# Float16 attention scores from tile 18 on, and five moves of DVE and ACT work, in a windowed attention with a SiLU MLP

## The chip, the cores and the metric

One core of a Trainium2 chip runs the kernel. The metric is the device time of one execution in microseconds, the median over several runs. The engines are TensorE (PE, its weight loads PEld), VectorE (DVE), ScalarE (ACT), GpSimd (POOL) and SyncE (SP), which issues the transfers here.

## The reference

Attention over 8 batches, 8 heads, 576 tokens, 64 numbers a head, with a causal window of 128 tokens and a bias that falls linearly with the distance; then a two-layer MLP with SiLU, from 512 to 2048 and back, over the 8 × 576 = 4608 tokens. Inputs and output are float32.

```python
scores = scale * np.matmul(q, k.transpose(0, 1, 3, 2))        # scale = 1/8
bias = slopes[:, None, None] * (-np.abs(rel))[None, :, :]
mask = (rel >= 0) & (rel < window)                            # window = 128
scores = np.where(mask, scores + bias[None], -1000000000.0)
scores = scores - np.max(scores, axis=-1, keepdims=True)
attn = np.exp(scores)
attn = attn / (np.sum(attn, axis=-1, keepdims=True) + 1e-09)
x = np.matmul(attn, v)           # (B, H, S, D), then to (4608, 512)
h = x @ w_in
g = h * (1.0 / (1.0 + np.exp(-h)))
out = g @ w_out
```

## The kernel before

**Tiles.** The tokens make 36 tiles of 128. Two batches (1152 tokens) are nine tiles, so four "two-batches" b = 0 to 3 follow each other; the first tile of each has no tile before it and only half of the score blocks (`blocks`), and the fifth is cut between two batches (`other_batch`, L301 to 308). A pair p is half of a tile's heads: i, q = divmod(p, 2), 72 pairs in all. A pair has two halves u of two heads h each.

**A pair's steps.** `scores` (L286 to 299): float32 matmuls of 64 rows, the two heads of a half on the two halves of the rows, 8 a full pair and 4 in a first tile; a float32 matmul leaves two records in the trace, so the profile counts x16 and x8. `row_max` (L310 to 319, one half u a call): a custom DVE instruction scales the scores by −0.125, subtracts the bias table `tab` and keeps the minimum of the negated scores. `exps` (L321, ACT). `p_hi` (L334, ACT) and `p_lo` (L339, DVE) split the probabilities into two float16 parts, `p_transpose` (L347) turns them by a DMA. `attend` (L372 to 387): 24 float16 matmuls of 65 columns, products of two-part values. `normalize` (L398 to 412, DVE), `x_hi` (L422, ACT) and `x_lo` (L124, DVE) give the MLP's input in two float16 parts, which another DMA transposes; for the first four tiles PE transposes it (`x_transpose`, L434 to 439), and their probabilities too (L357 to 368).

**The MLP.** Nine groups g of 512 tokens (4 tiles, 8 pairs), 16 slices f of 128 hidden columns each, n = 16 g + f. `gemm1` (two halves, L489 in float16 from g = 2, L494 before) gives h; SiLU is `act1` (tanh, ACT L502), `act2` (DVE L507), `act3` (ACT L515 or, in float16, L517: gh), `act4` (DVE L523 or POOL L122: the low part gl); `gemm2` (two halves, L555, gl last of each three) sums over the slices into four output banks, and `store` (L560 to 568) empties these at a group's end, each through a buffer, "io" for the first two, and to memory. "io" has two buffers.

**Weights.** They come as 64-bit numbers. `w_next` starts one slice of one weight: `w_split1`, `w_low3` (ACT L585, L592), and at the next three positions `w_join` (DVE L597), `w_hi` (ACT L607), `w_lo` (POOL). 32 such pieces are taken one after another, three ahead of the main loop, the others at half 0 of each step of g = 0. Later `w_stat` finds each weight's largest number, and `conv1`, `conv2`, `conv3` (ACT L635, DVE L641 and L647) turn each of 32 slices to two-part float16, a slice each four positions; `conv2`'s result takes an "io" buffer, too.

**Scales.** Each two-batches' values are scaled by a power of two: `vscale_load` and `vscale_reduce` (L156, L168, L171) take the largest of nine chunks, and `vscale_finish` (L184 to 213) combines them in three stages (a reduction over a row; a PE transpose L193 and small DVE steps L195 to 206; a PE broadcast L209 and a copy). The values then go to two float16 parts by `v_hi` (POOL L266) and `v_lo` (DVE L277), which `attend` reads.

**The order.** Every engine works in the order in which the program issues. A group has 64 positions: two halves of `gemm1` and `gemm2` of each slice; a negative position lies ahead of the main loop. `put(position, step)` and `later` fill a plan (L657 to 733), and `begin` issues what is due ahead of each position's matmuls. A pair's `scores` stand at n = `at(p)`, 8 p − 78 for p ≥ 16, so a pair each eight positions; the others are offsets from it: row maxima at n + 1 and n + 2, `attend` at n + 13 in the steady part.

Of the kernel before, what the change touches and what calls it, by code (L numbers as in the profile page):

```python
# [78 lines left out]
def tile_window_attention_then_silu_mlp(ctx, tc, qk, v, w_in, w_out, base8, out):  # L79
# [79 lines left out]
    def vscale_reduce(b, i):  # L159
        t = vred[b][i]  # L160
        if i == 0:
            vred[b]["m"] = pool.tile([P, VCH], F32, tag="vm", name=f"vmx{b}")
# [21 lines left out]
    def vscale_finish(b, stage):  # L184

        r, name = vred[b], "".join(str(c) for c in b) if isinstance(b, tuple) else b
# [3 lines left out]
        elif stage == 1:  # L190
# [16 lines left out]
        else:  # L207
            ps = ps_of(next_tag("misc"), f"vs{name}")
            nc.tensor.matmul(ps[:, 0:2], ones[:1, :], r["col"][:1, 1:3], start=True, stop=True)  # L209
# [36 lines left out]
    ks, qs, rvs, st = {}, {}, {}, {}  # L246

# [44 lines left out]

# [17 lines left out]
    def row_max(p, u):  # L310
        q, o = p % 2, blocks(p)
        n = (o.stop - o.start) * P
        st[p]["t"][u] = t = pool.tile([P, 2, 2 * P], F32, tag="t", bufs=3, name=f"t{p}_{u}")
        for h in range(2):
            nc.vector.tensor_tensor_reduce(  # L315
                out=t[:, h, 2 * P - n :], in0=st[p]["sp"][h][:, u, o].rearrange("p o c -> p (o c)"),
                in1=tab[:, 4 * q + 2 * u + h, 2 * P - n :], scale=-0.125, scalar=3.0e38,
# [344 lines left out]
    for p in range(NPAIR):  # L662
# [8 lines left out]
        else:  # L671
            a = n + (2 * STEP + 2 if p < 2 * GT else 15 if p < 4 * GT else 13)
# [4 lines left out]
        put(n + 2, row_max, p, 1)  # L677
# [27 lines left out]
        if q == 0:  # L705
            if i > 1:
# [8 lines left out]
    for x in range(3):  # L715
        for which in range(2):
# [153 lines left out]
```

## Time and profile before

| | |
|---|---|
| median of 3 runs | 969.84 us (969.56 to 971.48) |
| the profiled execution | 973.28 us |
| its span, first to last instruction | 971.5 us |
| mean granted PE clock | 0.988 of full speed |
| PE busy | 938.7 us |
| DVE, ACT, POOL busy | 597.0, 497.3, 141.6 us |

The page and the views give one profiled execution. In the timeline each row is a start, a busy time, an engine, a line, an operation, out<-in by the program's names, partitions × elements and a count; in brackets stands how long the engine was idle just before and what ended that. A row of matmuls merges neighbours, and its busy time includes the fill at the end, so that spacing is read from start to start. In a view of windows "PEclk" is the share of full clock that was granted. In a view of waits a row has the waiting engine and line, what it waited for, the total, how often, and the longest.

### The profile page before, as it was taken

How to read it: one execution, taken by the hardware profiler on the slowest of the kernel's cores; microseconds unless marked ns; L12 is line 12 of the kernel's file. 1: busy time of each engine (PE TensorE's matmuls, PEld its weight loads, DVE VectorE, ACT ScalarE, POOL GpSimd, SP SyncE). 2: the span in 40 equal slices, each digit the busy share in tenths (PEclk: the TensorE clock that was granted, in tenths of full speed). 3: DMA queues.
4: the chain of work that ended last, by engine and by line, in shares of the span. 5: the costliest groups of instructions: out<-in, count | busy, mean ns of one | idle time of the engine just before them, and what ended most of it. 6: DMA issues, size and time to landing. Idle time of an engine off the chain costs nothing.

```text
span 971.5 us, 17272 instructions
## 1 busy us (share of the span) xinstructions
PE 938.7 (97%) x6572; PEld 578.0 (59%) x6572; DVE 597.0 (61%) x1535; ACT 497.3 (51%) x1016; POOL 141.6 (15%) x129
## 2 busy tenths in 40 slices
PE   7989899999989999999999999999999999999998
PEld 5866677777768887544545554554555555544443
DVE  4867886656768877877566656555555565543222
ACT  4688877775544544555454445444544454433222
POOL 3146655122112222000000000000000000000000
PEclk8999999999998999999999999999999999999999
DMA  7949982333353542433364535333434343231001
GB/s 233 305 143 220 252 233 58 88 77 77 76 137 102 111 109 66 120 80 78 93 157 117 118 87 125 87 83 77 129 83 85 86 126 84 63 55 54 1 1 44
DMA packets 201075, 104.95 MB, mean 108 GB/s; under 512 B 168224, under 2 KB 176416, under 8 KB 200992
## 3 DMA queue, kind: packets, MB, share of 16 engines
q1 hardware_dynamic: 200992, 103.84, 42.1%
q8 instruction: 52, 0.85, 0.4%
q14 instruction: 31, 0.25, 0.1%
HBM read 54.00 MB, written 9.44 MB: 65 GB/s over the span
## 4 chain that ended last, share of the span: by engine, by line
PE 84%; DVE 5%; DMA 4%; ACT 4%; issue 2%; SPq 1%; POOL 0%; ACTq 0%; DVEq 0%; POOLq 0%
PE o L555 33%; PE h L489 30%; PE sp L295 7%; PE h L494 7%; PE av L385 5%; DMA vm<-v 1%; DMA early<-v 1%; DVE v L277 1%; DVE t L315 1%; DMA hl<-hr 1%; DVE gt L507 1%; DVE wm L597 1%; DMA wr<-w_out 1%; ACT gt L502 1%; PE pt L357 1%
## 5 line engine op out<-in xcount | busy, mean ns | idle before, releaser
L555 PE MATMUL o<-w,gh 128*128 128x512 f16 (+1 forms) x1152 | 351.7, 387 | 0.3 <-ACT gh L515 0.3
L489 PE MATMUL h<-xt,w 128*128 128x512 f16 (+1 forms) x1536 | 318.0, 355 | 0.0
L502 ACT ACTIVATE gt<-h,gsc 128x512 f32<-128x512 f32 x112 | 77.0, 687 | 319.6 <-PE h L489 317.6
L555 PE MATMUL o<-w,gl 128*128 128x512 f16 (+1 forms) x576 | 221.7, 385 | 1.5 <-POOL gl L122 1.5
L489 PEld LDWEIGHTS <-w 128*128 128x128 f16 x1536 | 143.8, 98 | 130.9 <-issue 2.4
L507 DVE SCALAR_TENSOR_TENSOR gt<-gt,h 128x512 f32<-128x512 f32 x144 | 98.6, 685 | 179.3 <-ACT gt L502 179.0
L555 PEld LDWEIGHTS <-gh 128*128 128x128 f16 x768 | 74.8, 98 | 88.6
L325 ACT ACTIVATE t<-t,mx 128x256 f32<-128x256 f32 (+1 forms) x288 | 121.4, 485 | 7.6 <-DVE mx L315 7.6
L315 DVE CUSTOM_DVE_ANT_0 t<-sp,tab 128x256 f32<-128x256 f32 (+1 forms) x288 | 102.2, 402 | 18.4 <-PE sp L295 18.0
L523 DVE SCALAR_TENSOR_TENSOR gl<-gt,gh 128x512 f16<-128x512 f32 x96 | 66.4, 691 | 75.0 <-ACT gh L517 74.9
L339 DVE SCALAR_TENSOR_TENSOR hr<-t,hr 128x512 f16<-128x512 f32 (+1 forms) x128 | 93.4, 747 | 24.4 <-ACT hr L334 24.4
L494 PE MATMUL h<-xh,w 128*128 128x512 f32 x256 | 91.6, 412 | 4.1 <-ACT xh L438 3.2
L266 POOL TENSOR_SCALAR v<-rv,vsc 128x512 f16<-128x512 f32 x32 | 26.7, 834 | 443.0 <-DMA rv<-v 311.7
L295 PEld LDWEIGHTS sp<-k,q 64*128 64x128 f32 x1088 | 69.4, 192 | 30.8 <-issue 30.1
L295 PE MATMUL sp<-k,q 64*128 64x128 f32 x1088 | 83.8, 291 | 3.6 <-DVE xs L412 3.5
L122 POOL TENSOR_TENSOR gl<-gt,gh 128x512 fp32r<-128x512 f32 x45 | 60.1, 1336 | 185.2 <-ACT gh L515 142.8
L517 ACT ACTIVATE gh<-gt 128x512 f16<-128x512 f32 x96 | 60.0, 625 | 47.5 <-DVE gt L507 47.2
L555 PEld LDWEIGHTS o<-w,gh 128*128 128x128 f32 x384 | 69.9, 188 | 16.5 <-ACT gh L515 1.2
L334 ACT ACTIVATE hr<-t 128x512 f16<-128x512 f32 (+1 forms) x128 | 75.9, 598 | 3.2 <-DMA hl<-hr 3.2
L385 PEld LDWEIGHTS <-hl 128*128 128x128 f16 x1632 | 58.7, 98 | 26.2 <-issue 15.4
L385 PE MATMUL av<-v,hl 128*128 128x65 f16 (+1 forms) x1632 | 63.3, 194 | 9.9 <-DVE mx L315 5.5
L555 PEld LDWEIGHTS <-gl 128*128 128x128 f16 x384 | 37.5, 98 | 47.8 <-DVE gl L523 3.5
(99 smaller groups left out, 786.6 us busy)
## 6 DMA issues: line engine op xcount, KB each, us to landing
q<-qk SPq DMA_DIRECT2D x36, 256.0 KB, 3.0
k<-qk SPq DMA_DIRECT2D x36, 256.0 KB, 3.1
out<-ot SPq DMA_DIRECT2D x36, 256.0 KB, 2.4
wr<-w_in SPq DMA_DIRECT2D x16, 512.0 KB, 6.6
wr<-w_out SPq DMA_DIRECT2D x16, 512.0 KB, 6.2
rv<-v SPq DMA_DIRECT2D x32, 256.0 KB, 2.9
vm<-v SPq DMA_DIRECT2D x27, 256.0 KB, 3.2
early<-v SPq DMA_DIRECT2D x9, 256.0 KB, 6.1
```

What stands on the lines that cost most here:

```text
L295: nc.tensor.matmul(sp[h][:, u, o], qs[i][rows, 2 * q + u], ks[i - 1 + o][rows, 2 * q + u], start=True, stop=True, skip_group_check=True,)
L315: nc.vector.tensor_tensor_reduce(out=t[:, h, 2 * P - n :], in0=st[p]["sp"][h][:, u, o].rearrange("p o c -> p (o c)"), in1=tab[:, 4 * q + 2 ...
L325: nc.scalar.activation(x, x, AF.Exp, bias=st[p]["mx"][:, 2 * u + h : 2 * u + h + 1], scale=-1.0)
L334: nc.scalar.activation(split_of(p, u, hr)[:, 0], t[:, :, 2 * P - n :], AF.Copy, scale=PSCALE)
L339: nc.vector.scalar_tensor_tensor(out=hr[:, 1], in0=t[:, :, 2 * P - n :], scalar=PSCALE, in1=hr[:, 0], op0=ALU.mult, op1=ALU.subtract)
L385: nc.tensor.matmul(av[:, 2 * u + h, : rhs.shape[-1]], lhs, rhs, start=(n == 0), stop=(n == len(seq) - 1), skip_group_check=True,)
L489: nc.tensor.matmul(o, w[:, wp, cc], x, start=start and k == 0, stop=stop, skip_group_check=True)
L494: nc.tensor.matmul(hps[n], w[:, cc], x, start=(half == 0 and i == 0), stop=(half == 1 and i == len(seq) - 1), skip_group_check=True,)
L502: nc.scalar.activation(gt, hps[n], AF.Tanh, scale=scale)
L507: nc.vector.scalar_tensor_tensor(out=gt, in0=gt, scalar=1.0, in1=hps[n], op0=ALU.add, op1=ALU.mult)
L523: nc.vector.scalar_tensor_tensor(out=gl, in0=gt, scalar=CUT, in1=gh, op0=ALU.mult, op1=ALU.subtract)
L555: nc.tensor.matmul(ops[ti], a[:, t], w, start=(f == 0 and i == 0), stop=(f == NF - 1 and i == len(seq) - 1), skip_group_check=True,)
```

## The change

1. From tile 18 on (p ≥ 36, b = 2 and 3) the scores are float16 products. A second input `qk16` holds q and k with each head's 64 rows on both halves of the partitions. `load_qk16` brings both for a pair (512 KB) at n − 18. `hi16` (ACT, n − 10 for q, n − 8 for k) scales them into float16, `lo16` (DVE, n − 6 and n − 5) takes the rest: for q into the upper 64 rows of the same tile, for k into a second one. A score block is then two matmuls of 128 rows, q's hi and lo against k's hi, and against k's lo: 16 matmuls of 128 columns for a full pair instead of 8 float32 ones. The scale of q and k goes into the bias table, which is multiplied once for each of the two two-batches (`rescale_bias`), and into the row maximum's scale, now a column.
2. For these scales `qk_load` and `qk_sum` (ACT, two sums of absolute values each) read the q and k of b = 2 and 3 ahead of time, and `scales16` combines them with the values' scale. The old loads of q and k from tile 18 on are gone.
3. `row_max` of the second half stands at n + 1, right behind the first's, for p ≥ 8.
4. The first three `w_next` stand at −25, −17 and −10 instead of −19, −7 and −2, and the fourth one position later.
5. The conversions of slices above 4 come three positions later (`CLEAR`).
6. The stages of the scales stand at 0, +2 and +5 instead of 0, +1 and +2; the two weights' scales share their instructions (`wscale_finish`).
7. `attend` stands at n + 12 instead of n + 13 for p ≥ 36.

The core of the diff:

```diff
+QK16 = 2
+CLEAR = 3
...
+    def qk_sum(b, i):
+        t = vred.pop((b, "qk", i))
+        for k in range(2):
+            m = vred[b]["m"][:, (1 + k) * VCH + i : (1 + k) * VCH + i + 1]
+            nc.scalar.activation(t[:, k], t[:, k], AF.Abs, accum_out=m)
...
+    def rescale_bias(b):
+        ratio = vsc[b][:, 8:9] if b > QK16 else vsc[b][:, 7:8]
+        flat = tab.rearrange("p h c -> p (h c)")
+        nc.vector.tensor_scalar_mul(flat, flat, ratio)
...
+    def load_qk16(p):
+        i, q = divmod(p, 2)
+        raw16[p] = t = pool.tile([P, 2, 4, P], F32, tag=RAW16[p % 2], bufs=1, name=f"r16_{p}")
+        nc.sync.dma_start(t, qk16[i - QK16 * NBLK, q])
...
+        nc.scalar.activation(out16, raw16[p][:, k], AF.Copy, scale=scale)
...
+        rows = slice(D, P) if k == 0 else slice(0, P)
+        hi, lo = (q16[p], q16[p]) if k == 0 else (k16[i][:, q, 0], k16[i][:, q, 1])
+        nc.vector.scalar_tensor_tensor(
+            out=lo[rows], in0=raw16[p][rows, k], scalar=vsc[i // NBLK][rows, 2 + 2 * k : 3 + 2 * k], in1=hi[rows],
+            op0=ALU.mult, op1=ALU.subtract,
+        )
...
+                if i >= QK16 * NBLK:
+                    for h in range(2):
+                        for part in range(2):
+                            nc.tensor.matmul(
+                                sp[h][:, u, o], q16[p][:, 2 * u + h], k16[i - 1 + o][:, q, part, 2 * u + h],
+                                start=part == 0, stop=part == 1, skip_group_check=True,
+                            )
+                    continue
...
+        scale = vsc[b][:, 6:7] if b >= QK16 else -0.125
...
-            a = n + (2 * STEP + 2 if p < 2 * GT else 15 if p < 4 * GT else 13)
+            a = n + (2 * STEP + 2 if p < 2 * GT else 15 if p < 4 * GT else 13 if i < QK16 * NBLK else 12)
+        if i >= QK16 * NBLK:
+            put(n - 18, load_qk16, p)
+            put(n - 10, hi16, p, 0)
+            put(n - 8, hi16, p, 1)
+            put(n - 6, lo16, p, 0)
+            put(n - 5, lo16, p, 1)
+            if block_of(i) == 0 and q == 0:
+                put(n, rescale_bias, i // NBLK)
...
-        put(n + 2, row_max, p, 1)
+        put(n + (2 if p < 2 * GT else 1), row_max, p, 1)
...
+    for x, wait in enumerate((0, 2, 5)):
+        put(STATS + 2 * NF + 2 + wait, wscale_finish, x)
...
-                put(n + SLICE * f + (k if which or f else 0), fn, which, f)
+                put(n + SLICE * f + (CLEAR if f > 4 else 0) + (k if which or f else 0), fn, which, f)
...
+            if b >= QK16:
+                put(n - 52 + 5 * i, qk_load, b, i)
+                put(n - 46 + 5 * i, qk_sum, b, i)
...
-        for n in (-19, -7, -2):
+        for n in (-25, -17, -10):
...
-                if g == 0 and half == 0:
+                if g == 0 and half == (n == 0):
```

On PE before, the scores of pair 40 (tile 20), between a `gemm2` and a `gemm1`; sp40_0 and sp40_1 are the banks of the two heads, k19 and k20 the tiles of k:

```order
L555 MATMUL o3_3_4974<-w16_1_5_5232,gl59_5641 128x512
L295 MATMUL sp40_0_5725<-k19_5080,q20_5352 128x128
L295 MATMUL sp40_1_5726<-k19_5080,q20_5352 128x128
L295 MATMUL sp40_0_5725<-k20_5354,q20_5352 128x128
L295 MATMUL sp40_1_5726<-k20_5354,q20_5352 128x128
L295 MATMUL sp40_0_5725<-k19_5080,q20_5352 128x128
```

The same place on PE after:

```order
L682 MATMUL o3_3_4991<-w16_1_5_5330,gl59_5713 128x512
L413 LDWEIGHTS q16_40_5622
L413 MATMUL sp40_0_5801<-k16_19_5382,q16_40_5622 128x128
L413 LDWEIGHTS q16_40_5622
L413 MATMUL sp40_0_5801<-k16_19_5382,q16_40_5622 128x128
L413 LDWEIGHTS q16_40_5622
L413 MATMUL sp40_1_5802<-k16_19_5382,q16_40_5622 128x128
L413 LDWEIGHTS q16_40_5622
L413 MATMUL sp40_1_5802<-k16_19_5382,q16_40_5622 128x128
```

Each float32 matmul has become two float16 ones into the same bank, each with its own weight load; the place in the order is the same.

On DVE before, at the row maxima of pair 15 (g = 0); wm10_1 is the weight piece being joined, gt10 the SiLU of slice 10:

```order
L315 ISA t15_0_1790,mx15_1775<-sp15_0_1765,tab_65 128x256
L315 ISA mx15_1775 128x1
L315 ISA t15_0_1790,mx15_1775<-sp15_1_1766,tab_65 128x256
L315 ISA mx15_1775 128x1
L597 SCALAR_TENSOR_TENSOR wm10_1_1787<-wm10_1_1787,wr10_1_1361 128x512
L315 ISA t15_1_1809,mx15_1775<-sp15_0_1765,tab_65 128x256
L315 ISA mx15_1775 128x1
L315 ISA t15_1_1809,mx15_1775<-sp15_1_1766,tab_65 128x256
L315 ISA mx15_1775 128x1
L507 SCALAR_TENSOR_TENSOR gt10_1807<-gt10_1807,h10_1780 128x512
```

The same on DVE after:

```order
L442 ISA t15_0_1790,mx15_1775<-sp15_0_1765,tab_65 128x256
L442 ISA mx15_1775 128x1
L442 ISA t15_0_1790,mx15_1775<-sp15_1_1766,tab_65 128x256
L442 ISA mx15_1775 128x1
L442 ISA t15_1_1793,mx15_1775<-sp15_0_1765,tab_65 128x256
L442 ISA mx15_1775 128x1
L442 ISA t15_1_1793,mx15_1775<-sp15_1_1766,tab_65 128x256
L442 ISA mx15_1775 128x1
L724 SCALAR_TENSOR_TENSOR wm10_1_1787<-wm10_1_1787,wr10_1_1364 128x512
L634 SCALAR_TENSOR_TENSOR gt10_1810<-gt10_1810,h10_1780 128x512
```

The join has moved from between the two halves of the maxima to behind them.

On DVE before, at the end of g = 1; ot1_1 and ot1_3 are output tiles, wr16_0_5 and w16_0_2 belong to the conversion of slice 5 of the first weight, xs24 and x12 to the attention of tile 12:

```order
L565 TENSOR_SCALAR ot1_1_3446<-o1_1_2391 128x512
L339 SCALAR_TENSOR_TENSOR hr25_1_3427<-t25_1_3403,hr25_1_3427 128x512
L641 SCALAR_TENSOR_TENSOR wr16_0_5_3477<-w0_5_1188,vscw0_2999,w16_0_2_3370 128x512
L565 TENSOR_SCALAR ot1_3_3488<-o1_3_2409 128x512
L403 TENSOR_SCALAR r24_3491<-av24_3449 128x4
L404 RECIPROCAL r24_3491<-r24_3491 128x4
L647 SCALAR_TENSOR_TENSOR w16_0_2_3370<-w0_5_1188,vscw0_2999,wr16_0_5_3477 128x512
L412 TENSOR_TENSOR xs24_3510<-av24_3449,r24_3491 128x256
```

The same on DVE after:

```order
L692 TENSOR_SCALAR ot1_1_3433<-o1_1_2391 128x512
L466 SCALAR_TENSOR_TENSOR hr25_1_3415<-t25_1_3371,hr25_1_3415 128x512
L692 TENSOR_SCALAR ot1_3_3473<-o1_3_2409 128x512
L530 TENSOR_SCALAR r24_3476<-av24_3436 128x4
L531 RECIPROCAL r24_3476<-r24_3476 128x4
L539 TENSOR_TENSOR xs24_3496<-av24_3436,r24_3476 128x256
L130 SCALAR_TENSOR_TENSOR x12_3513<-xs24_3496,x12_3513 128x256
L768 SCALAR_TENSOR_TENSOR wr16_0_5_3527<-w0_5_1188,vscw_3046,w16_0_2_3358 128x512
```

The conversion's second step has moved from ahead of the normalizing of pair 24 to behind it.

More of the change, by code (lines that the diff above doesn't have):

```diff
@@ L184, in vscale_finish @@
     def vscale_finish(b, stage):
[L186 removed]
+        if b >= QK16:
+            scales16(b, stage)
+            return
+        r, name = vred[b], b
         if stage == 0:
@@ new lines, in rescale_bias, with wscale_finish @@
+    def rescale_bias(b):
+        ratio = vsc[b][:, 8:9] if b > QK16 else vsc[b][:, 7:8]
+        flat = tab.rearrange("p h c -> p (h c)")
+        nc.vector.tensor_scalar_mul(flat, flat, ratio)
+    def wscale_finish(stage):
+        if stage == 0:
+            vred["w", "col"] = col = pool.tile([P, 3], F32, tag="vcol", name="vcolw")
+            for k in range(2):
+                nc.vector.tensor_reduce(col[:, k : k + 1], vred["w", k]["m"], axis=AX.X, op=ALU.max)
+        elif stage == 1:
+            ps = ps_of(next_tag("misc"), "vtw")
+            for k in range(2):
+                nc.tensor.transpose(ps[:1, k * P : (k + 1) * P], vred["w", "col"][:, k : k + 1], ident)
+            vred["w", "row"] = row = pool.tile([P, 9], F32, tag="row", bufs=1, name="roww")
+            c, inv = row[:1, 0:2], row[:1, 2:4]
+            ci = c.bitcast(I32)
+            nc.vector.tensor_reduce(c, ps[:1, : 2 * P].rearrange("p (k i) -> p k i", k=2), axis=AX.X, op=ALU.max)
+            nc.vector.tensor_single_scalar(ci, ci, 0x7F800000, op=ALU.bitwise_and)
+            nc.vector.tensor_single_scalar(ci, ci, 1, op=ALU.logical_shift_right)
+            nc.vector.tensor_single_scalar(ci, ci, 0x1FC00000, op=ALU.add)
+            nc.vector.tensor_single_scalar(ci, ci, 0x7F800000, op=ALU.bitwise_and)
+            nc.vector.tensor_single_scalar(inv.bitcast(I32), ci, -(14 << 23), op=ALU.add)
+            nc.vector.tensor_scalar(ci, ci, -1, 268 << 23, op0=ALU.mult, op1=ALU.add)
+        else:
+            ps = ps_of(next_tag("misc"), "vsw")
+            nc.tensor.matmul(ps[:, 0:4], ones[:1, :], vred["w", "row"][:1, 0:4], start=True, stop=True)
+            t = pool.tile([P, 4], F32, tag="wsc", bufs=1, name="vscw")
+            nc.vector.tensor_copy(t, ps[:, 0:4])
+            for k in range(2):
+                wsc["w", k] = t.rearrange("p (s k) -> p k s", k=2)[:, k]
```

94 lines of the change are left out of this document (75 added, 19 removed).

## The prediction

> **What bounds the kernel now.** I read the page first: the busy shares, the granted clock and the chain that ended last.
>
> ```profile
> span 971.5 us, 17272 instructions
> PE 938.7 (97%) x6572; PEld 578.0 (59%) x6572; DVE 597.0 (61%) x1535; ACT 497.3 (51%) x1016; POOL 141.6 (15%) x129
> PEclk8999999999998999999999999999999999999999
> PE 84%; DVE 5%; DMA 4%; ACT 4%; issue 2%; SPq 1%; POOL 0%; ACTq 0%; DVEq 0%; POOLq 0%
> ```
>
> TensorE (PE) is busy for 97% of the span, and 84% of the last chain is its own work. Time can be won by cheaper TensorE work, fewer waits of it, and less time at half clock. An early and a steady stretch tell where its waits are (columns: stretch, its length, busy time of PE, PEld, DVE, ACT, POOL, then granted clock, DMA share, GB/s).
>
> ```profile
> 62.00:128.00 66.00, 60.33 (x413) 46.62 (x413) 51.70 (x119) 53.70 (x107) 36.71 (x27) 0.97 0.96 235
> 490.00:589.00 99.00, 98.81 (x708) 50.47 (x706) 63.16 (x177) 44.78 (x90) 3.80 (x4) 1.00 0.52 120
> ```
>
> The early stretch loses 5.7 us on PE, with DVE at 78% and ACT at 81%. The steady one loses 0.2 of 99 us, with DVE at 64% and ACT at 45%. There only the price of PE's own work matters, as long as the others keep up. PE's waits, by what ended them (total us, times, longest):
>
> ```profile
> PE av L385 <- DVE mx L315: 5.5, 5, 2.4
> PE av L385 <- DVE v L277: 4.1, 8, 1.2
> PE sp L295 <- DVE xs L412: 3.5, 1, 3.5
> PE h L494 <- ACT xh L438: 3.2, 1, 3.2
> PE vs L209 <- DVE vcol L206: 2.3, 2, 1.2
> PE vsw L209 <- DVE vcolw L206: 0.9, 1, 0.9
> ```
>
> All the sums below are against the profiled execution, 973.28 us with its span of 971.5. The median of the three timed runs, 969.84, is 3.4 us below it.
>
> **The change, part by part.** *Scores.* A score block of a full pair in the timeline (start, busy, engine, line, operation), and a half block, of the first tile of two batches:
>
> ```profile
> 563.12 1.46 PE L489 MATMUL h<-xt,w 128*128 128x512 f16 x6
> 564.41 0.89 PE L385 MATMUL av<-v,hl 128*128 128x65 f16 x24
> 565.14 1.46 PE L489 MATMUL h<-xt,w 128*128 128x512 f16 x6
> ...
> 568.81 0.38 PE L555 MATMUL o<-w,gl 128*128 128x512 f16 x1
> 569.12 1.16 PE L295 MATMUL sp<-k,q 64*128 64x128 f32 x16
> 570.21 2.76 PE L489 MATMUL h<-xt,w 128*128 128x512 f16 x12
> ```
> ```profile
> 422.53 0.38 PE L555 MATMUL o<-w,gl 128*128 128x512 f16 x1
> 422.84 0.72 PE L295 MATMUL sp<-k,q 64*128 64x128 f32 x8
> 423.49 1.25 PE L489 MATMUL h<-xt,w 128*128 128x512 f16 x5
> ```
>
> From start to start, six float16 matmuls of 512 columns take 564.41 − 563.12 = 1.29 us, 215 ns each, and 24 of 65 columns take 565.14 − 564.41 = 0.73, 30.4 ns each, with a weight load for every one. The block between L555's last matmul (568.81 + 0.215) and L489's next (570.21) takes 1.18 us; the half block takes 0.74. The new block has 16 float16 matmuls of 128 columns, 8 in a half block. On the line between 65 and 512 columns one of them is worth 30.4 + 63 × (215 − 30.4)/447 = 56.4 ns, so the blocks are worth 0.90 and 0.45. From tile 18 on there are 32 full and 4 half pairs: 32 × 0.28 + 4 × 0.29 = **−10.1 us**. The bounds come from the weight loads, which are as many as the matmuls:
>
> ```profile
> L385 PEld LDWEIGHTS <-hl 128*128 128x128 f16 x1632 | 58.7, 98 | 26.2 <-issue 15.4
> ```
>
> One is recorded at 98 ns; were none hidden, 32 × 16 + 4 × 8 = 544 of them would take 53.3 us where the old blocks take 32 × 1.18 + 4 × 0.74 = 40.7: **+12.6**. But 24 matmuls with 24 loads went by in 0.73 us, 30 ns a pair, so I take the line. The other end, −11.5, has no overhead at all: 215/512 × 128 = 54 ns a matmul. The Trainium skill, "TensorE: Matmul & The Clock Gate", section "Back-to-back issue gap", speaks against this part: a sustained stream of weight load and matmul has, it says, about 81 ns a matmul at 128 columns and about 131 at 512. By it the blocks would take 544 × 81 ns = 44.1 us, an estimate, so the scores would cost 3.4 us more instead of 10.1 less. The trace departs from its second figure: 215 ns at 512 columns.
>
> *Row maxima in one step.* The longest of L385's five waits for a row maximum ends behind these two steps of DVE:
>
> ```profile
> 120.73 1.36 DVE L597 SCALAR_TENSOR_TENSOR wm<-wm,wr 128x512 int32<-128x512 int32 x1
> 122.01 0.41 DVE L315 CUSTOM_DVE_ANT_0 t<-sp,tab 128x256 f32<-128x256 f32 x1
> ```
>
> A weight join (L597) stands on DVE between the two halves of pair 15's maxima and holds the second back by 122.01 − 120.73 = 1.28 us. L385 waits since its output bank is one that the maxima still read. With the halves side by side the join goes behind them, so this wait falls to 2.4 − 1.28 = 1.1. The other four add up to 5.5 − 2.4 = 3.1, each shorter than such a join on average (0.78), and could go whole: 1.28 + 3.1 = 4.4. Not every join will have stood as long as this one, so I take **−4.0** (all 5.5 gone; half of it, 2, where the join then delays the weights). Behind the long wait PE ran at half clock:
>
> ```profile
> 122.60:125.80 3.20, 3.20 (x29) 2.81 (x30) 1.70 (x6) 2.59 (x6) 1.28 (x1) 0.50 0.97 215
> 378.00:381.00 3.00, 3.00 (x45) 2.78 (x46) 2.96 (x6) 0.46 (x1) 1.56 (x1) 1.00 0.39 87
> ```
>
> The second row follows a wait of 1.1 us and has full clock. With 1.1 left, the 3.2 × 0.5 = 1.6 us should come back: **−1.5** (0 to −1.6).
>
> *Conversions clear of the stores.* At the end of the second group (g = 1):
>
> ```profile
> 287.89 0.75 DVE L641 SCALAR_TENSOR_TENSOR wr<-w,vscw,w 128x512 f32<-128x512 f32 x1 [3.94 <-DMA out<-ot]
> ```
>
> And the stretch behind it:
>
> ```profile
> 290.60:296.50 5.90, 5.86 (x33) 4.56 (x34) 5.35 (x15) 1.58 (x3) 1.29 (x1) 0.50 0.32 99
> ```
>
> The conversion L641 needs a buffer that an output store still reads, and DVE stands for 3.94 us. Queued behind it is L412, whose reading frees the bank that the scores of pair 26 want, so PE stands for the 3.5 us of the waits, and then runs 5.9 us at half clock: 5.9 × 0.5 = 2.95. Three positions later, L641 comes behind L412 and x's low part. Both costs go, 3.5 + 2.95 = 6.4. Behind it now is the next SiLU step (L507); I give back 1.1, a third of the stall: **−5.3** (−3.5 to −6.4).
>
> *Ends of groups.* L385 waited 4.1 us in eight places for the values' low part (L277). In the first three groups' ends a second half of row maxima stood ahead of it; its two steps of 0.41 us (122.01, above) are up to 0.8 less at each, of which I count 0.65 for not always being last: 3 × 0.65 = **−1.9** (0 to −2.4). From tile 18 on, attend is one position earlier, and so is L277, but the last low half of SiLU stays where it is:
>
> ```profile
> 488.69 0.69 DVE L523 SCALAR_TENSOR_TENSOR gl<-gt,gh 128x512 f16<-128x512 f32 x1 [0.70 <-ACT gh L517]
> ...
> 489.99 0.74 DVE L277 SCALAR_TENSOR_TENSOR v<-rv,vsc,v 128x512 f16<-128x512 f32 x1
> 490.79 0.76 PE L385 MATMUL av<-v,hl 128*128 128x64 f16 x20 [0.19 <-DVE v L277]
> ```
>
> L277 can't be much ahead of this, and a matmul that is due a position (99/64 = 1.5 us) sooner finds it late by what the maxima beside it, 0.8 less, don't make good, 1.5 − 0.8 = 0.7. I count 0.65 at three of the four ends that are left: **+2.0** (0 to +3).
>
> *Scales spread.* Two of the three waits of L209, 1.1 of the 2.3 and the 0.9 for the weights, have a chain of small DVE steps in them, with PE queued behind. Three positions between the stages cover them: **−2.0** (−1.5 to −2.0).
>
> *Weights sooner.* The third weight's splits (L585, L592) stand on ACT just ahead of the cast of the transposed x (L438), for which L494 waits 3.2 us, once. The splits go to positions where ACT and DVE are still at the first pairs' probabilities, and hold those up instead; I count 3 us lost against 3.2 won: **+0.3**, from −3 to +3.
>
> *What is added.* Each pair from tile 18 on gets two conversions on ACT and two on DVE, and each of two batches gets 18 sums on ACT, two for each of nine loads. The nearest rows, and that of a load as large as a pair's q and k, in place of the smaller ones of before:
>
> ```profile
> L635 ACT ACTIVATE w<-w,vscw 128x512 f16<-128x512 f32 x31 | 22.1, 712 | 0.0
> L647 DVE SCALAR_TENSOR_TENSOR w<-w,vscw,wr 128x512 f16<-128x512 f32 x31 | 25.4, 820 | 0.0
> wr<-w_in SPq DMA_DIRECT2D x16, 512.0 KB, 6.6
> ```
>
> The load is issued eight positions, 12 us, ahead of its conversion, so ACT and the SiLU steps queued there don't wait for 6.6 us. The work is 2 × 0.71 = 1.4 us of ACT and 2 × 0.82 = 1.6 of DVE a pair, in the 99/8 = 12.4 us of a pair in the steady stretch (a group of eight). What covers it is the slack of the SiLU chain:
>
> ```profile
> 564.14 0.69 DVE L523 SCALAR_TENSOR_TENSOR gl<-gt,gh 128x512 f16<-128x512 f32 x1 [1.28 <-ACT gh L517]
> ...
> 566.87 0.38 PE L555 MATMUL o<-w,gl 128*128 128x512 f16 x1
> ```
>
> gl is ready at 564.83 and wanted at 566.87: 2.0 us. Most additions fall apart from each other and are covered; for places where both fall in one chain, the rescaled bias (128x2048, on DVE, twice) and the busier SP queue (DMA share now 0.52) I take **+2** (0 to +6).
>
> Sum: −10.1 − 4.0 − 1.5 − 5.3 − 1.9 + 2.0 − 2.0 + 0.3 + 2 = −20.5. That is 973.28 − 20.5 = 952.8 on the profiled execution's scale, and 969.84 − 20.5 = **949 us** on the median's.
>
> **The rivals.** *Returned waits* (0.12). Only the cheaper scores last: each wait removed comes back at the next bank, as the 5.7 us lost at 62 to 128 were with DVE and ACT at some 80%. Then −10.1 for the scores, and about +3 of the +4 for attend and the additions: 969.84 − 7 = about 963. Against it: the 3.94 us stall has one cause, a buffer. *Dear matmuls* (0.05). The float16 blocks run at a third above my price, since a load (98 ns) hides only in part behind a 128-column matmul (56 ns); midway between the two is 77 ns. 544 × 77 ns = 41.9 us, 1.2 more than the old blocks: the sum loses 10.1 + 1.2 = 11.3 and comes to about 961. (The page's 81 ns, an estimate of the Trainium skill, would make it 963.) Against it: the 30 ns a pair. *Late SiLU, slower* (0.06). The conversions come in one queue with L502, L507, L517 and L523, all ahead of gl. From tile 18 on, the chain can slip by the 2.0 us of slack and by the 0.57 that a pair has won (20.5/36) before the kernel is slower than it was; the added work of a pair that stands in it decides. All of it is 1.4 + 1.6 = 3.0 us, past the point of 2.6: 1.0 us late (3.0 − 2.0) in each of 36 pairs is +36, so 969.84 − 20.5 + 36 = about 985. Against it: DVE and ACT there are 64% and 45% busy, and the four conversions sit at four different positions. My forecast keeps 0.77.
>
> **How the numbers follow.** With every term at its better end the sum is −11.5 − 5.5 − 1.6 − 6.4 − 2.4 + 0 − 2.0 − 3 + 0 = −32, 938 us; with every one at its worse (the scores at −10.1) −10.1 − 2 − 0 − 3.5 − 0 + 3 − 1.5 + 3 + 6 = −5, 965. They won't all fall to one side: the forecast alone goes some two thirds of the way, 942 to 959. The range takes in the first two rivals, 961 and 963: **942 to 964**. Left out are late SiLU and some 0.1 at both ends. A measurement of this kernel can tell about 0.2% from no change, 2 us. Faster by more than that: the forecast and the first two rivals, 0.94, less 0.04 where loads are less hidden than in any of them or upper bounds meet: 0.90. Of that, 0.03 is within 0.2% and 0.01 joins late SiLU: slower 0.07.
>
> **What would show it.** The float16 score block at 0.9 us from neighbour to neighbour (1.2 or more would be the dear matmuls); no wait above 1.2 us of L385 for a row maximum; full clock from 120 to 300 us; the conversions behind x's low part with no PE wait near 287; waits of the early attends up to 1 us at the last groups' ends; PE above 98.5% busy from 490 to 590. Wrong would be a steady stretch with waits of L555 for gl, or a start whose first GEMM1 comes over 3 us later than now.

## The result, and the profile after

The changed kernel takes 962.32 us (median of 4 runs, 960.08 to 963.50) against 970.66 for the kernel before (4 runs, 969.56 to 973.49): a ratio of 0.9907, with a 95% interval of 0.9878 to 0.9936. It is faster by 8 to 9 us, not by the 20.5 of the prediction. Run again beside the experiments, the ratio was 0.9887 (0.9866 to 0.9909), or 11 us. The time lies in the predicted range and the sign is right; the size is some 0.4 of the forecast in the first measurement and about half of it in the second.

The page of the changed kernel:

```profile
span 958.3 us, 17430 instructions
PE 924.9 (97%) x6574; PEld 576.1 (60%) x6574; DVE 662.7 (69%) x1610; ACT 562.2 (59%) x1160; POOL 144.4 (15%) x129
PEclk8998999999999999999999999999999999999999
```

PE's own work fell by 938.7 − 924.9 = 13.8 us, by its busy time. DVE and ACT have 65 us more to do each, and PE still is busy for 97%. The profiled executions lie further apart than the medians, 973.28 and 960.08 us, since one is among the longer runs of its kernel and the other among the shorter. PE's waits, longest first:

```profile
PE av L512 <- DVE v L395: 5.6, 6, 1.3
PE sp L420 <- DVE xs L539: 4.7, 1, 4.7
...
PE av L512 <- POOL v L393: 2.0, 1, 2.0
...
PE av L512 <- DVE mx L442: 1.7, 2, 1.2
PE pt L484 <- DVE hl L495: 1.6, 1, 1.6
```

The waits for the row maxima (mx) have gone from 5.5 to 1.7, the two for L209 in the steady part and the one for the cast of x (xh) are gone. But the wait of the scores for the normalizing (xs) is there again, 4.7 us long, and two of the start are new (POOL v, hl). To see where, I compared the start of a SiLU step (DVE's L507, L634 after) on both sides; n counts the slices of the hidden layer, 16 a group:

| n | before, us | after, us | difference | predicted up to here |
|---|---|---|---|---|
| 0 | 57.33 | 59.39 | +2.1 | |
| 4 | 87.06 | 92.18 | +5.1 | |
| 16, end of first group | 180.65 | 183.48 | +2.8 | −5.9 |
| 36 | 317.04 | 312.76 | −4.3 | −12.7 |
| 48 | 400.15 | 394.97 | −5.2 | −14.5 |
| 143, the last | 962.34 | 949.81 | −12.5 | −20.5 |

The table ends 4 us better than the medians differ (8.3), since it compares the two executions named above. In them, the change brings 15.4 us from n = 16 on, where 14.6 were predicted. What is missing there is missing in the first group: a loss of 2.8 us, where the prediction had a gain of 5.9 (weights +0.3, row maxima −4.0, clock −1.5, and a third of the −1.9 for the values). In the windows, the first of these is the stretch that lost 5.7 us on PE before:

```profile
62.00:128.00 66.00, 58.90 (x404) 45.88 (x405) 51.79 (x114) 51.97 (x103) 39.70 (x28) 0.95 0.88 220
82.70:89.50 6.80, 3.90 (x19) 3.31 (x20) 5.16 (x9) 5.69 (x11) 3.08 (x3) 0.50 0.99 238
120.00:300.00 180.00, 175.47 (x1177) 138.28 (x1177) 121.57 (x289) 123.04 (x274) 60.31 (x47) 1.00 0.51 120
490.00:589.00 99.00, 97.59 (x725) 51.67 (x723) 77.99 (x202) 66.69 (x144) 3.69 (x4) 1.00 0.74 192
```

It now loses 7.1, and from 82.7 to 89.5 us, the end of the long wait and the work behind it, the granted clock was 0.50. From 120 to 300 us the clock is full, as predicted.

**The new stall.** Its chain in the timeline, from SP's loads to PE's scores:

```profile
70.20 0.34 SPq L380 DMA_DIRECT2D rv<-v  x1
...
73.10 4.05 SPq L474 DMA_TRANSPOSE hl<-hr  x1
...
82.58 0.63 ACT L461 ACTIVATE hr<-t 128x512 f16<-128x512 f32 x1 [4.56 <-DMA hl<-hr]
83.24 0.69 DVE L466 SCALAR_TENSOR_TENSOR hr<-t,hr 128x512 f16<-128x512 f32 x1 [4.12 <-ACT hr L461]
...
85.04 0.41 DVE L539 TENSOR_TENSOR xs<-av,r 128x256 f32<-128x256 f32 x1
...
85.61 2.04 PE L420 MATMUL sp<-k,q 64*128 64x128 f32 x14 [4.69 <-DVE xs L539]
```

To be read from below: the scores want a bank that DVE's normalizing reads (L539); that is queued behind the probabilities' low part (L466), which waits for ACT's high part (L461), which waits for a buffer that a transposing DMA still reads. Ahead of that DMA SP issued six loads in a burst from 70.20 to 72.53 (v, q, k, two weights, a chunk of v), 2 MB in all by their sizes (512 KB for each weight, 256 for the rest), and then the transposes. That the burst makes them late is a reading of this order; numbers 3, 13 and 14 below test it. From 64 to 88 us the landing of the transposes took (first the kernel after; second the kernel before, from 62 to 86):

```profile
DMA to landing us min/median/max: 3.1/3.3/9.4
```
```profile
DMA to landing us min/median/max: 2.8/4.6/7.0
```

The kernel before had such a wait of ACT, too, 3.2 us at 80.23, but L412 (the normalizing) had run ahead of it, at 78.39. There, nobody on PE waited for it:

```profile
78.39 0.42 DVE L412 TENSOR_TENSOR xs<-av,r 128x256 f32<-128x256 f32 x1
...
80.23 0.63 ACT L334 ACTIVATE hr<-t 128x512 f16<-128x512 f32 x1 [3.19 <-DMA hl<-hr]
```

**The scores** came out as predicted:

```profile
562.10 0.38 PE L682 MATMUL o<-w,gl 128*128 128x512 f16 x1
562.32 1.06 PE L413 MATMUL sp<-k,q 128*128 128x128 f16 x16
563.21 2.75 PE L616 MATMUL h<-xt,w 128*128 128x512 f16 x12
```

From 562.10 + 0.215 to 563.21 a block takes 0.89 us (forecast 0.90, before 1.18): 56 ns a matmul, its weight load hidden.

### The profile page after: what moved, and what is told of

Same layout as the page of the kernel before. It is cut to its first block, busy times and chain, and to the rows that moved or that the text cites. A ratio compares the mean times of both kernels' runs of the same rounds, so it can differ in the third digit from the quotient of the medians.

```text
span 958.3 us, 17430 instructions
## 1 busy us (share of the span) xinstructions
PE 924.9 (97%) x6574; PEld 576.1 (60%) x6574; DVE 662.7 (69%) x1610; ACT 562.2 (59%) x1160; POOL 144.4 (15%) x129
## 4 chain that ended last, share of the span: by engine, by line
PE 78%; DVE 3%; ACT 3%; issue 1%; POOL 1%; DMA 0%; ACTq 0%; DVEq 0%; POOLq 0%; SPq 0%
PE o L682 34%; PE h L616 29%; PE h L621 6%; PE av L512 4%; PE sp L413 3%; PE sp L420 2%; DVE gt L634 1%; ACT t L452 1%; DVE v L395 1%; POOL gl L128 1%; ACT gt L629 1%; ACT gh L642 0%; DMA vm<-v 0%; ACT hr L461 0%; ACT gh L644 0%
## 5 line engine op out<-in xcount | busy, mean ns | idle before, releaser
L616 PE MATMUL h<-xt,w 128*128 128x512 f16 (+1 forms) x1536 | 310.6, 353 | 0.0
L634 DVE SCALAR_TENSOR_TENSOR gt<-gt,h 128x512 f32<-128x512 f32 x144 | 98.5, 684 | 122.0 <-ACT gt L629 121.7
L466 DVE SCALAR_TENSOR_TENSOR hr<-t,hr 128x512 f16<-128x512 f32 (+1 forms) x128 | 95.9, 751 | 26.7 <-ACT hr L461 26.0
L650 DVE SCALAR_TENSOR_TENSOR gl<-gt,gh 128x512 f16<-128x512 f32 x96 | 66.3, 691 | 51.1 <-ACT gh L644 48.7
L461 ACT ACTIVATE hr<-t 128x512 f16<-128x512 f32 (+1 forms) x128 | 75.9, 598 | 5.7 <-DMA hl<-hr 5.7
L512 PEld LDWEIGHTS <-hl 128*128 128x128 f16 x1632 | 58.4, 98 | 25.6 <-issue 15.4
L442 DVE CUSTOM_DVE_ANT_0 t<-sp,tab,vsc 128x256 f32<-128x256 f32 (+1 forms) x144 | 58.6, 462 | 9.3 <-PE sp L413 8.8
L130 DVE SCALAR_TENSOR_TENSOR x<-xs,x 128x256 f16<-128x256 f32 x64 | 43.9, 686 | 23.8 <-ACT x L549 23.7
L621 PEld LDWEIGHTS h<-xh,w 128*128 128x128 f32 x256 | 48.5, 190 | 13.7 <-DVE xl L566 1.2
```

The lines of the kernel that those rows point to most:

```text
L461: nc.scalar.activation(split_of(p, u, hr)[:, 0], t[:, :, 2 * P - n :], AF.Copy, scale=PSCALE)
L466: nc.vector.scalar_tensor_tensor(out=hr[:, 1], in0=t[:, :, 2 * P - n :], scalar=PSCALE, in1=hr[:, 0], op0=ALU.mult, op1=ALU.subtract)
L512: nc.tensor.matmul(av[:, 2 * u + h, : rhs.shape[-1]], lhs, rhs, start=(n == 0), stop=(n == len(seq) - 1), skip_group_check=True,)
L616: nc.tensor.matmul(o, w[:, wp, cc], x, start=start and k == 0, stop=stop, skip_group_check=True)
L621: nc.tensor.matmul(hps[n], w[:, cc], x, start=(half == 0 and i == 0), stop=(half == 1 and i == len(seq) - 1), skip_group_check=True,)
L634: nc.vector.scalar_tensor_tensor(out=gt, in0=gt, scalar=1.0, in1=hps[n], op0=ALU.add, op1=ALU.mult)
```

## The experiments

Thirteen edits of the changed kernel, and as number 5 the changed kernel itself again. Times are medians over at least four runs, and the ratio is that to the kernel before, measured beside them. As the kernel before came to 972.4 to 973.5 us there and to 970.7 in the first measurement, ratios are compared, not times; the changed kernel stands at 0.9907 and 0.9887, so a difference from it is given as a range.

| kernel | us | ratio (95%) |
|---|---|---|
| 5 changed, again | 961.89 | 0.9887 (0.9866 to 0.9909) |
| 1 old first weights | 955.81 | 0.9826 (0.9809 to 0.9843) |
| 2 old row maxima | 965.12 | 0.9926 (0.9904 to 0.9948) |
| 3 one load back | 957.88 | 0.9854 (0.9836 to 0.9872) |
| 4 attend at n + 13 | 962.02 | 0.9893 (0.9875 to 0.9911) |
| 6 float32 scores | 969.66 | 0.9967 (0.9951 to 0.9982) |
| 7 scores only | 971.20 | 0.9984 (0.9970 to 0.9999) |
| 8 conversions back | 965.56 | 0.9928 (0.9909 to 0.9947) |
| 9 fourth weight later | 954.60 | 0.9810 (0.9793 to 0.9826) |
| 10 values early | 957.04 | 0.9832 (0.9815 to 0.9848) |
| 11 both | 950.42 | 0.9770 (0.9754 to 0.9787) |
| 12 old weights, old maxima | 961.19 | 0.9877 (0.9860 to 0.9894) |
| 13 chunk loads later | 963.22 | 0.9908 (0.9884 to 0.9933) |
| 14 all three | 953.60 | 0.9806 (0.9780 to 0.9832) |

**1. The first weights put back.**

```diff
-        for n in (-25, -17, -10):
+        for n in (-19, -7, -2):
-                if g == 0 and half == (n == 0):
+                if g == 0 and half == 0:
```

> The changed kernel with the weights' splits back at their old positions (-19, -7, -2, and half 0 of every step). Theory A (one weight load that the change has put behind three other loads makes SP issue a burst at 70 to 72.5 us; the probabilities' transposes queue behind it, ACT waits 4.6 us for their buffer, DVE's normalizing and PE's scores stand behind that, then half clock): the 4.7 us wait of the scores near 80 us goes with 2 us of half clock, 962 - 7 = 955 us or less. Theory B (the row maxima in one step stand ahead of the reduction that frees the value buffer, so SP's burst comes from that): the wait of the scores near 80 us stays at 4 us or more, 960 to 962. Besides, the first tanh comes 2 us sooner by both, but a wait of GEMM1 of 3 us for the cast of x returns near 50 us.

Its waits of PE:

```profile
PE h L621 <- ACT xh L565: 3.2, 1, 3.2
PE av L512 <- DVE mx L442: 2.4, 2, 1.6
PE sp L420 <- DVE xs L539: 1.8, 1, 1.8
```

0.9826: 6 to 8 us faster than the changed kernel. The wait of the scores fell to 1.8, and the 3.2 us of GEMM1 for the cast of x came back. At n = 16 it stands at −1.1 us in the table above (+2.8 after). So the new positions of the weight pieces together cost more than the wait they remove: this part of the change is a loss. Numbers 3 and 9 take it apart.

**2. The row maxima in two steps.**

```diff
-        put(n + (2 if p < 2 * GT else 1), row_max, p, 1)
+        put(n + 2, row_max, p, 1)
```

> The changed kernel with the second half of the row maxima back one position later. Theory A (the load): the 4.7 us wait of the scores near 80 us stays; the waits of attend for the row maxima come back, 4 us: 964 to 967. Theory B (the maxima ahead of the reduction): the wait near 80 us goes (-7), the old waits come back (+4): 958 to 960.

```profile
PE av L512 <- DVE mx L442: 10.4, 7, 2.2
...
PE sp L420 <- DVE xs L539: 2.3, 1, 2.3
```

0.9926, 2 to 4 us slower than the changed kernel, and +9.0 us at n = 16 in the profiled execution, which at 969.49 us is its longest. The wait for the normalizing fell to 2.3, by neither theory; it neither stayed at 4.7 nor went (number 5 shows that this wait differs from execution to execution). Theory B, the maxima as the root, fails by the time: it said 958 to 960 us, and the kernel took 965.12.

**3. One load put back.** The changed condition at half 0 moves the sixth weight piece one position later, not only the fourth; this undoes the sixth.

```diff
-                if g == 0 and half == (n == 0):
+                if g == 0 and half == (n == 0 and k == "g1"):
```

> The changed kernel with only the sixth weight piece's split one position earlier, at half 0 of its step as before the change, so that the load of the second weight's slice 6 stands between the two transposes of pair 8 again, not behind the loads of v, q and k. Theory A (that load): the wait near 80 us falls below 1.5 us, 962 - 7 = 955. Theory B (the maxima): it stays at 4 us or more, 961 to 963.

On SP before, where that load (wr6_1) stands between the two transposes of pair 8; rv, q and k are the next tile's loads:

```order
L347 DMA_TRANSPOSE hl8_0_943<-hr8_0_924 128x8x128
L580 DMA wr6_1_962<-w_out 128x1024
L347 DMA_TRANSPOSE hl8_1_973<-hr8_1_941 128x8x128
L262 DMA rv5_980<-v 128x512
L257 DMA q6_982<-qk 128x512
L253 DMA k6_984<-qk 128x512
L575 DMA wr8_0_1006<-w_in 128x4x256
```

After, it is part of the burst:

```order
L474 DMA_TRANSPOSE hl8_0_940<-hr8_0_923 128x8x128
L474 DMA_TRANSPOSE hl8_1_970<-hr8_1_938 128x8x128
L380 DMA rv5_980<-v 128x512
L375 DMA q6_982<-qk 128x512
L371 DMA k6_984<-qk 128x512
L707 DMA wr6_1_987<-w_out 128x1024
L702 DMA wr8_0_1005<-w_in 128x4x256
```

With it back, no wait of the scores for the normalizing is left in PE's waits, and the ratio is 0.9854: so the place of this one piece, and of the load that it issues, is worth 3 to 5 of the 6 to 8 us that the first experiment won. This kernel still has the two new waits of the start (2.0 and 1.6 us). That the place of the load decides alone is not shown: numbers 1, 9 and 11 have it back as well and still wait there.

**4. Attend one position later.**

```diff
-13 if i < QK16 * NBLK else 12)
+13)
```

> The changed kernel with attend back at n + 13 for pairs 36 on. If the four waits of attend at the ends of groups 3 to 6 (1.06 us each by the spacing of matmuls, 0.35 to 0.93 before) come from attend's earlier position while the values' low part comes when it did, they fall to 0.4 or less: 962 - 2.3 = 960. If they come from the row maxima or the added conversions on DVE, they stay: 962.

```profile
PE o L682 <- DVE gl L650: 2.3, 4, 1.0
```

0.9893, the same as the changed kernel. The waits at the ends did shrink, from 1.06 to 0.57 at three of four, but four new ones for the low part of SiLU (gl) came, 2.3 us where the changed kernel has 0.5. The expectation of 2.3 us was wrong: the earlier attend is neither the loss that I took it for nor a gain.

**6 and 7. The scores taken out, and the scores alone.** Number 5 is the changed kernel itself, in the table's first row.

> The changed kernel again, unedited, beside the three that follow on the same chip: 0.991 of the kernel before, with the wait of the scores near 80 us again at 3.5 to 5 us if it comes from the order of SP's queue, and gone in this run if it was one execution's chance.

Its wait of the scores near 80 us was 2.4 us. In the other executions of the same first group it was 4.7 (above), 3.6 (number 4), 4.7 (number 6), 2.7 (number 8) and 2.9 (number 10): always there, but of no fixed size. And its granted clock falls in two places where the profile above has full clock, though not behind the wait of the scores, which ends at 84.95:

```profile
46.30:49.70 3.40, 3.40 (x37) 2.99 (x35) 0.82 (x3) 0.00 (x0) 0.36 (x1) 0.50 0.69 263
63.40:66.80 3.40, 3.30 (x16) 2.46 (x18) 2.51 (x3) 3.40 (x8) 3.08 (x4) 0.50 0.06 14
84.00:93.00 9.00, 7.37 (x60) 5.68 (x61) 6.63 (x18) 6.86 (x14) 4.10 (x4) 1.00 0.93 241
```

Both come behind waits of PE that the kernel before doesn't have or has shorter (1.6, 0.7 and 2.0 us up to 45.5; 1.5 us at 62.1, 0.3 before). Numbers 2, 3, 4, 6, 8 and 10, which start alike, have such a pair of stretches, too; number 13 has none, like the profile above. As 3.4 us at 0.50 are 1.7 us of full clock lost, the table above shows less than what this start mostly costs. Number 6:

```diff
-QK16 = 2
+QK16 = 4
-13 if i < QK16 * NBLK else 12)
+13 if i < 2 * NBLK else 12)
```

> The changed kernel with float32 scores for all tiles, so without the conversions, the sums, the rescaled bias and their loads; attend stays at n + 12. If the scores are worth what their blocks show (0.89 us against 1.18, 36 times) and the added ACT and DVE work is covered, it is 10 us slower than the changed kernel. If the added work takes back a part of it, it is slower by 4 to 7 only.

0.9967 against 0.9887: 7.8 us slower. From n = 36 on, number 5 gains 8.0 us on the kernel before and number 6 loses 0.3, a difference of 8.3: the blocks are worth 36 × 0.29 = 10.4, so about 2 of it goes into the added work. Number 7 has everything but the scores put back (the edits of numbers 1, 2, 4 and 8, and the scales' stages at 0, +1, +2).

> The changed kernel with everything but the float16 scores put back (the weights' splits, the row maxima, attend at n + 13, the conversions, the scales' stages; the shared weight scales stay). Scores worth 10 with covered additions: 9 to 10 us below the kernel before, 0.990 of it, and the start as before, so as fast as the whole change by itself. If additions cost: 5 us or less below.

```profile
PE vs L263 <- DVE row L260: 3.9, 2, 2.8
```

0.9984: 2 us, not 9. From n = 36 on this kernel gains nothing on the kernel before (it loses 0.3 us), where number 5 gains 8.0. The scales' chain on DVE now has nine small steps (0.14 to 0.54 us, one of 1.17) with PE queued behind, 3.9 us in two waits where the kernel before has one of 1.1, and behind the longer one, at 378 us, PE runs 3.4 us at 0.50. The values come later at the groups' ends, too: attend's waits there are 1.2 to 1.8 us, 0.8 or less before. So in these traces the float16 scores are worth 8 us beside the other moves, and nothing without them. The trace points at the spread stages and the joined maxima; as five edits were put back at once, the share of each is not shown.

**8. The conversions put back.**

```diff
-CLEAR = 3
+CLEAR = 0
```

> The changed kernel with the conversions at their old positions. The step of the prediction (the store's buffer holds DVE and so the scores at the end of the second group, then half clock) says 4 to 6.5 us slower than the changed kernel, with a wait of the scores of about 3.5 us near 285 us. If the wait had been given back behind the moved conversion, or comes from the row maxima's order, it is slower by under 2.

```profile
290.63 0.75 DVE L768 SCALAR_TENSOR_TENSOR wr<-w,vscw,w 128x512 f32<-128x512 f32 x1 [3.81 <-DMA out<-ot]
...
293.38 1.83 PE L420 MATMUL sp<-k,q 64*128 64x128 f32 x13 [3.53 <-DVE xs L539]
```
```profile
293.00:300.00 7.00, 6.62 (x38) 5.15 (x38) 5.38 (x16) 1.65 (x3) 1.27 (x1) 0.52 0.74 255
```

0.9928 against 0.9887, 4 us; from n = 16 to the end, 9.9 us are gained where number 5 gains 15.1, so 5.2. Stall and half clock are back, both as in the prediction.

**9, 10 and 11. Toward a faster kernel.** Number 9 is the first experiment with only the fourth piece later; number 10 is the changed kernel with the values' two parts two positions earlier from tile 18 on; number 11 has both.

```diff
-        for n in (-25, -17, -10):
+        for n in (-19, -7, -2):
-                if g == 0 and half == (n == 0):
+                if g == 0 and half == (n == 0 and k == "g1"):
```
```diff
-            put(a - 3, v_hi, i)
-            put(a - 2, v_lo, i)
+            put(a - (3 if i < QK16 * NBLK else 5), v_hi, i)
+            put(a - (2 if i < QK16 * NBLK else 4), v_lo, i)
```

> The first three weights' splits at their old positions (-19, -7, -2) as in the first experiment, and only the fourth one position later, behind the last two casts of the transposed x. Two of the four splits that stand on ACT ahead of these casts (0.56 + 0.55 us) go, so GEMM1's wait of 3.2 us near 50 us falls to 2.1, and the kernel is 1 us below the first experiment's, 0.981 of the kernel before. If the start's cost in the changed kernel came from the fourth split and not from the first three, it is slower than the first experiment by 2 or more.

> The changed kernel with the values' two parts (POOL, DVE) two positions earlier from tile 18 on, ahead of the SiLU step that stands before them on DVE. If attend's four waits of 1.06 us at the ends of groups 3 to 6 come from that step, they fall below 0.3: 3 to 4 us below the changed kernel, 0.985 of the kernel before. If the low part of SiLU then comes late, the gain is 1 or less.

> The two edits before together: the changed kernel with the first three weights' splits put back, the fourth one position later, and the values' parts earlier from tile 18 on. As they touch different stretches the gains add up: 0.977 to 0.979 of the kernel before, about 950 us, and faster than the changed kernel by 10 or more.

In number 9 the wait for the cast fell from 3.2 to 2.1 and the ratio to 0.9810; against the first experiment's 0.9826 that is 1.6 us, with intervals that overlap. From number 3 it differs in the first three pieces alone, and there the difference is clear: 0.9810 against 0.9854, 3 to 4 us. In the changed kernel the wait at a group's end looked like this:

```profile
482.58 0.69 DVE L650 SCALAR_TENSOR_TENSOR gl<-gt,gh 128x512 f16<-128x512 f32 x1 [0.70 <-ACT gh L644]
...
483.19 0.74 DVE L395 SCALAR_TENSOR_TENSOR v<-rv,vsc,v 128x512 f16<-128x512 f32 x1
...
483.99 0.76 PE L512 MATMUL av<-v,hl 128*128 128x64 f16 x20 [0.90 <-DVE v L395]
```

In number 10 L395 stands ahead of that L650, and the waits are down to two, both in the first group:

```profile
PE av L512 <- DVE v L395: 2.0, 2, 1.3
```

0.9832, 5 to 7 us below the changed kernel; from n = 48 on it gains 10.9 us where the changed kernel gains 7.3. Both together give 950.42 us and 0.9770: 11 to 13 us faster than the changed kernel, and 2.3% faster than the kernel before.

**12. Old weights and old maxima.**

> The first experiment with the second half of the row maxima back one position later. The prediction's step says that side by side they are worth 4 us in the first group and 2 in the others: 6 us slower than the first experiment. If in the first group each wait only gives way to the next, only the ends of groups 3 to 6 show it (0.6 each): 2 to 2.5 slower.

0.9877 against 0.9826: the maxima in one step are worth 5 us, with the weights as before. But where? In the two profiled executions, 4.4 us apart, this kernel stands at −0.5 at n = 16 and the first experiment at −1.1: 0.6 us in the first group. The other 3.8 come from n = 16 on, at the ends of groups, where the spacing of matmuls shows waits of 1.68 here and 1.06 there at the last four, and 0.7 at two earlier ones that the first experiment lacks.

**13 and 14. The chunk loads moved.** The nine chunks of v for the next scale were read at positions −2 to 38, beside everything else; here at 14 to 38. They share their buffers with the value loads, so SP stands at rv until DVE has reduced a chunk. Number 13 leaves the weight load of number 3 where the change put it; number 14 has the same edit on number 11.

```diff
-            put(n - 54 + 5 * i, vscale_load, b, i)
-            put(n - 50 + 5 * i, vscale_reduce, b, i)
+            put(n - 38 + 3 * i if b == 1 else n - 54 + 5 * i, vscale_load, b, i)
+            put(n - 34 + 3 * i if b == 1 else n - 50 + 5 * i, vscale_reduce, b, i)
```

> The changed kernel with the nine value chunks of the second two batches loaded and reduced at positions 14 to 42 (one each three) instead of -2 to 42 (one each five), so none of them between 60 and 80 us. If SP standing at the value load until DVE has reduced a chunk, and the burst behind it, makes the transposes late (their landing took up to 9.4 us), the wait of the scores near 80 us falls from 2.4 to 4.7 us to under 1, and the kernel is 3 to 6 us faster than the changed one, 0.983 to 0.986. If the place of the weight load alone makes it, the wait stays above 2 us: 0.988 to 0.991.

> The fastest kernel so far (weights' splits back, the fourth one later, values early) with the same later chunk loads. If the chunks are the root, its wait of 2.1 us near 78 us goes: 0.974 to 0.975 of the kernel before. If not: 0.977 as before, or slower where the chunks now crowd the end of the first group.

In number 13 the wait near 80 us is gone, and from 60 to 90 us the transposes landed faster:

```profile
DMA to landing us min/median/max: 3.0/3.5/4.4
```

At n = 4 it stands at +0.4 (changed: +5.1). But then DVE waits for the chunks themselves, at 104 and again at 129 us, and the scores with it:

```profile
105.47 0.69 DVE L174 TENSOR_REDUCE vmx<-vm 128x1 f32<-128x512 f32 x1 [1.68 <-DMA vm<-v]
...
106.67 0.42 DVE L539 TENSOR_TENSOR xs<-av,r 128x256 f32<-128x256 f32 x1
...
107.24 1.13 PE L420 MATMUL sp<-k,q 64*128 64x128 f32 x14 [3.08 <-DVE xs L539]
```

At n = 16 it is at +3.0 again, and the ratio is 0.9908. Number 14 lost 3 us to number 11. Number 14 has no wait of the scores near 78 us either, and also one at 104. So the chunks belong to the cause of the stall at 80 us, since taking them out of that stretch removes it with the weight load in place; but at the place tried here, the stall moves with them.

## Why the prediction was right or wrong

**Right in mechanism and size.** The scores, −10.1: 0.89 us a block, 36 × 0.29 = −10.4. The rule of the Trainium skill that spoke against it ("TensorE: Matmul & The Clock Gate", section "Back-to-back issue gap", about 81 ns a matmul at 128 columns) doesn't hold here: 56 ns. The conversions, −5.3: 5.2 by number 8. The values at the first ends of groups, −1.9: the waits at 282 and 393 us (0.5 each) are gone, and the 0.6 and 1.2 near 174 became one of 1.3, so about 1.6. The last ends, +2.0: by the spacing of matmuls four waits of 1.06 where there were 0.35, 0.93, 0.35 and 0.35, +2.3; but number 4 shows that the later attend would have cost as much elsewhere. The scales, −2.0: the weights' wait went and the one near 378 us fell from 1.27 to 0.15 by spacing, about 2. The added work, +2: about 2 by number 6. What was taken as separate terms depends on each other more than the sum says: number 7, with the scores alone, is 2 us faster than the kernel before, not 9.

**Wrong: weights sooner, +0.3, in truth a loss of 4 to 8 us** (6 to 8 by number 1, 4 to 5 by number 2 against number 12). The step counted 3 us lost against 3.2 won at the start. The 3.2 were won, as the wait for the cast is gone, but the start came out 2.1 us late at n = 0 all the same. The step named ACT and DVE, and forgot POOL, the last step of the same weight piece:

```profile
42.74 1.26 POOL L128 TENSOR_TENSOR w<-wm,w 128x512 fp32r<-128x512 f32 x1 [18.26 <-ACT w L734]
43.98 0.69 POOL L384 TENSOR_SCALAR v<-early,vsc 128x512 f16<-128x512 f32 x1
...
46.91 0.76 PE L512 MATMUL av<-v,hl 128*128 128x64 f16 x20 [1.99 <-POOL v L393]
```

The values that attend waits for stand on POOL behind the weight's low part, and that waits for ACT's cast of the weight. In the kernel before, the same step on the values ran 12 us earlier:

```profile
31.85 0.69 POOL L266 TENSOR_SCALAR v<-early,vsc 128x512 f16<-128x512 f32 x1 [7.15 <-PE av L385]
```

And the step didn't follow the loads that each piece issues: the sixth piece's move, which the list of the change doesn't name, put one 512 KB load behind three others on SP, and the transposes behind a burst. The experiments give the parts: the first three pieces cost 3 to 4 us (number 9 against 3), the sixth 3 to 5 (number 3), and the fourth by itself wins about 1.6 (number 9 against 1, not clear of the noise).

**Wrong: row maxima −4.0 and clock −1.5 in the first group, in truth about 1 us or nothing.** The waits for the maxima did fall as computed (5.5 to 1.7, or 2.4 in number 1). But the first group has waits that take each other's place, as the rival "returned waits" said, in its own stretch: number 1 waits 1.8 us for the normalizing near 80 us, where the kernel before doesn't wait. Single executions differ too much at n = 16 to price this (0.6 by numbers 12 and 1, 3.7 to 6.5 by number 2's longest execution against the six of the changed first group), so I estimate it from the times: 5.0 us between numbers 12 and 1 less 3.8 behind n = 16 leaves 1.2; 2 to 4 us between number 2 and the changed kernel less 3.0 to 3.3 behind n = 16 leaves −1 to 1. The joined maxima are worth 3 to 4 us all the same, but behind n = 16, at the ends of the later groups, which the prediction had priced at 1.3 net of the first.

The clock step named a real cost. Of the four executions with the maxima in two steps, three ran 3.4 us at 0.50 behind that wait: the kernel before, number 2 (from 131.5) and number 12; number 7, which waits 1.5 us there, did not. None of the others has half clock behind a wait for the maxima.

```profile
122.00:125.40 3.40, 3.40 (x29) 3.01 (x30) 1.83 (x6) 2.61 (x6) 1.28 (x1) 0.50 1.10 299
```

This is number 12. What the prediction left out is that new waits bring half clock to new places, at the start and behind the stall: from 20 to 180 us the mean granted clock is 0.98 in the kernel before, 0.96 to 0.98 in the six executions of the changed first group, and 0.99 and 1.00 in numbers 9 and 11.

**What stays open.** Numbers 9 and 11 have the load of number 3 in its old place, and still 3.3 and 2.1 us of wait near 80 us, where number 3 has none. Executions of the same first group differ by 2.8 us at n = 16 (+2.5 to +5.3 over six); half clock that comes and goes is a part of this, but not in step with it (0.98 goes with +2.5, 0.97 with +2.8 and +5.3, 0.96 with +3.8 to +4.7). Of the kernel before there is one trace only. How the transfers of that stretch share the engines, I can't tell from these traces. A third buffer for the transposes' source, which might take ACT's wait away by itself, wasn't tried.

## What to carry to other kernels

When a step is moved, write down each instruction and each transfer that it sets off, engine by engine, and look at what they now stand ahead of in each queue; here splits on ACT brought a POOL step ahead of the values and a load ahead of the transposes, and these two cost more than the wait that was removed. Where two engines and the transfers are all near 80% or more, as from 62 to 128 us here, a removed wait is worth what the next one leaves, not its length: price it from another execution or at zero, and keep the full price for stretches in which one engine is the bound. And a low part that is late at a group's end is cheaper to issue two positions early than to move its reader.

## What the runs showed of the hardware

The custom row maximum is slower with a column as its scale than with a constant. The same 128x256 form, in one execution, with the constant (tiles below 18) and with the column:

```profile
L442 DVE CUSTOM_DVE_ANT_0 t<-sp,tab,vsc 128x256 f32<-128x256 f32 x128 | 53.9, 476 | 9.0 <-PE sp L413 8.8
L442 DVE CUSTOM_DVE_ANT_0 t<-sp,tab 128x256 f32<-128x256 f32 x128 | 46.4, 415 | 2.6 <-PE sp L420 2.6
```

That is 61 ns each, 0.24 us a pair, on an engine with room for it. The kernel before and number 6, with the constant for all tiles, have 417 over both ranges, so the tiles don't make the difference; the float16 scores come with the column in every run, and aren't shown apart from it. A conversion of 64 rows (L361, 777 ns) is no cheaper than one of 128 (749). And the clock doesn't follow the length of a single wait. Behind 2.4 us up to 122.6 the kernel before ran 3.2 us at 0.50, behind 2.4 us up to 85.0 number 5 ran on at 1.00, and so did number 13 behind a wait of 3.1 us, longer than either:

```profile
107.20:114.00 6.80, 6.76 (x59) 5.58 (x60) 5.68 (x14) 4.88 (x11) 3.20 (x3) 1.00 1.01 249
```

From 20 to 180 us, half clock came in stretches of about 3.4 or 6.8 us in these traces.
